# One wait of the wide exponential, and the places of some VectorE work, in a fused attention and token-mixing kernel

## The chip, the cores and the metric

The kernel runs on one core of a Trainium2 chip. A core has engines that run side by side, each through its own list of instructions in order: TensorE (PE; its weight loads are shown apart as PEld), VectorE (DVE), ScalarE (ACT), GpSimd (POOL), and SyncE (SP), which here only issues DMAs. An instruction can wait for semaphores that other engines, DMAs or its own engine raise. Whatever stands behind a waiting instruction on its engine waits as well. The metric is the time of one execution on the device in microseconds (us); lower is better.

## The reference

Two branches on the same x (2048 tokens of 512 channels, fp32) are mixed by a gate for each token:

```python
g = sigmoid((x * gate_w).sum(-1, keepdims=True))
q, k, v = split(x @ wqkv)                       # 32 heads of 16
p = softmax(q @ k.T * 16**-0.5)                 # per head, 2048 x 2048
a = concat_heads(p @ v) @ wo
h = layernorm(x)                                # over channels
u = gelu(h.T @ w1 + b1)                         # over tokens, 2048 -> 1792
b = (u @ w2 + b2).T                             # 1792 -> 2048
out = g * a + (1 - g) * b
```

Everything is fp32. Products are made of two rounded parts, hi and lo, of each factor (hi*hi + hi*lo + lo*hi).

## The kernel before

**Stages.** Until about 280 us the kernel makes v, the keys, half of the queries and the first layer of the token branch. From then to about 1255 us it runs attention, with the rest of the dense work beside it, and then a short end.

**A phase.** Attention is a loop over 128 phases `p`. Four phases (`ph` 0 to 3) make a group of two heads for 1024 queries (32 groups; groups 0 to 15 are the first half of the queries). Each phase computes 16 blocks of scores, 128 keys by 512 queries, numbered `n`. All become exponentials, in three ways:

- SINGLE, n = 0, 2, 4, 6, 8, 9: ScalarE takes each alone from PSUM (`p<-s`, L1043).
- TWO, (10, 11) and (12, 13): ScalarE takes two neighbouring banks at once (`p<-t`, L986, 1024 columns).
- EVAC, n = 1, 3, 5, 7, 14, 15: VectorE copies them to SBUF (`pe<-s`, and `pe<-u` for 14 and 15, L1039), and ScalarE turns all six into exponentials with one instruction, the wide exponential (`pe<-pe`, L1050, 3072 columns; in the last phase two parts of 1024 and 2048).

Then TensorE multiplies the exponentials with v (`av`, L921): first those that were held back in the phase before (the six of EVAC), then the ten of this phase. VectorE adds the result to `ot` (L943). In each phase with `ph` = 0 the group before is finished: its `ot` goes to memory in eight DMAs (`o`, `r`), and a second add (`ot<-t`) belongs to the new group.

**Dense work beside the scores.** A score uses 64 of the 128 rows of the array; the other 64 do a step of a dense product (`dn`, L1031), 12 or 14 steps a phase, one half of the contraction in an even and the other in the odd phase. The dense products are the second layer (16 tiles), 8 late projections of the queries' second half (`late_query`), and 8 tiles of the output projection of the first half (`project`). Each ends in an odd phase with VectorE reading the bank `dn` (`done`, for a late projection `out`, L605); the next phase's first step of `dn` needs that bank again.

**Order.** All five engines run in the order in which the program calls them (`manual_schedule`). In a phase, VectorE does the four copies `pe<-s`, the two `pe<-u`, then `done` of a dense product, a memset of `mark`, which stands for several waits at once, up to two casts of weights (in odd phases), what `on_dve(p, ...)` has put down for that phase (`later`), and then the adds. SyncE's DMAs of `call(p, ...)` are issued at the head of phase p. The tables of numbers below `put_whole` decide at which phase each piece runs. `tc.add_manual_dep(a, b, ...)` makes a wait for the end of b. The wide exponential has such a wait for `pairs_done[1]`, the second pair, the instruction just ahead of it on ScalarE; after it, later instructions need no own wait for that pair.

**Inversions and fetches.** The sums of exponentials go to memory (`r`), come back as `inv`, are inverted on VectorE (`invert`: `turn`, L734 and L735) and go back as `ri` (`put_back`). A fetch (L747) loads `o` and `ri`, multiplies them (`on_dve` at its first number), casts the product to hi (second number) and subtracts for lo (third). `fetch_left` runs four times, between phases 83 and 105; `fetch_right` and `fetch_o` from phase 112 on.

## Time and profile before

| what | value |
|---|---|
| median of 3 runs | 1290.22 us (1289.85 to 1290.26) |
| the profiled execution | 1290.4 us |
| its span in the profile | 1288.5 us |
| TensorE / ScalarE / VectorE / GpSimd busy | 1273.4 / 1084.4 / 854.2 / 199.2 us |
| wide exponentials | 129, the first at 283.5 us |
| granted clock of TensorE over the span | 0.999 |

The profile is of one execution. A timeline row reads: start and duration in us, engine, line of the kernel, operation, tiles written and read with their shapes, how many instructions are merged in the row, and in brackets the idle time of the engine ahead of it and what ended it. A row of waits reads: who waited for whom, us in total, how often, the longest. A row of windows reads, for a stretch: its length, the busy time of PE, PEld, DVE, ACT and POOL with instruction counts, the granted clock, the share of the DMA engines, GB/s. Consecutive instructions of an engine may overlap at their ends, so the time from start to start is what an engine needs for each.

### The profile page before, as it was taken

How to read it: one execution, taken by the hardware profiler on the slowest of the kernel's cores; microseconds unless marked ns; L12 is line 12 of the kernel's file. 1: busy time of each engine (PE TensorE's matmuls, PEld its weight loads, DVE VectorE, ACT ScalarE, POOL GpSimd, SP SyncE). 2: the span in 40 equal slices, each digit the busy share in tenths (PEclk: the TensorE clock that was granted, in tenths of full speed). 3: DMA queues.
4: the chain of work that ended last, by engine and by line, in shares of the span. 5: the costliest groups of instructions: out<-in, count | busy, mean ns of one | idle time of the engine just before them, and what ended most of it. 6: DMA issues, size and time to landing. Idle time of an engine off the chain costs nothing.

```text
span 1288.5 us, 32655 instructions
## 1 busy us (share of the span) xinstructions
PE 1273.4 (99%) x13342; PEld 846.5 (66%) x13342; DVE 854.2 (66%) x1547; ACT 1084.4 (84%) x1405; POOL 199.2 (15%) x316
## 2 busy tenths in 40 slices
PE   9999999999999999999999999999999999999998
PEld 7888888875666666666666666666656656666656
DVE  5675544088767666767667677766776677678873
ACT  4443344279999999999999999999999999999990
POOL 0220444461110101010110101111111111000000
PEclk9999999999999999999999999999999999999999
DMA  3799442253754443634344443444543342266511
GB/s 131 261 330 332 131 124 90 81 135 107 209 126 98 83 96 75 162 77 100 84 100 95 97 95 63 91 96 75 111 99 75 77 97 59 55 163 180 142 57 69
DMA packets 100554, 152.30 MB, mean 118 GB/s; under 512 B 17109, under 2 KB 56171, under 8 KB 96300
## 3 DMA queue, kind: packets, MB, share of 16 engines
q1 hardware_dynamic: 99820, 149.08, 45.0%
q8 instruction: 107, 1.75, 0.6%
q10 hardware_dynamic: 576, 1.05, 0.2%
q14 instruction: 51, 0.42, 0.1%
HBM read 105.39 MB, written 44.68 MB: 116 GB/s over the span
## 4 chain that ended last, share of the span: by engine, by line
PE 92%; DVE 4%; ACT 2%; DMA 1%; issue 1%; SPq 0%; DVEq 0%; ACTq 0%
PE av L921 26%; PE s L1022 19%; PE acc L424 12%; PE t L1022 9%; PE acc L75 8%; PE dn L1031 6%; PE t L921 5%; PE u L1022 3%; PE pa L1105 2%; DVE pe L1039 1%; ACT pe L1050 1%; PE acc L199 1%; ACT p L1043 1%; DVE row L610 0%; DVE row L68 0%
## 5 line engine op out<-in xcount | busy, mean ns | idle before, releaser
L1043 ACT ACTIVATE p<-s 128x512 f32<-128x512 f32 x768 | 388.4, 605 | 5.0 <-PE s L1022 2.8
L1050 ACT ACTIVATE pe<-pe 128x3072 f32<-128x3072 f32 x129 | 354.5, 2749 | 5.1 <-DVE mark L1058 1.0
L1022 PE MATMUL s<-qs,ks 64*128 64x512 f32 x1280 | 335.5, 403 | 3.7 <-DVE ot L943 3.5
L1039 DVE COPY pe<-s 128x512 f32<-128x512 f32 x512 | 318.0, 684 | 5.2 <-PE s L1022 1.6
L1022 PEld LDWEIGHTS s<-qs,ks 64*128 64x128 f32 x1280 | 224.8, 184 | 102.1 <-issue 48.6
L986 ACT ACTIVATE p<-t 128x1024 f32<-128x1024 f32 x256 | 254.3, 1076 | 0.0
L921 PE MATMUL av<-p,v 128*32 128x256 f32 x3880 | 227.2, 379 | 0.0
L1039 DVE COPY pe<-u 128x512 f32<-128x512 f32 x256 | 165.0, 686 | 85.5 <-PE u L1022 73.8
L921 PE MATMUL av<-pe,v 128*32 128x256 f32 x3072 | 192.5, 383 | 0.1
L943 DVE TENSOR_TENSOR ot<-av,ot 128x512 f32<-128x512 f32 (+2 forms) x149 | 91.3, 614 | 145.4 <-PE av L921 144.3
L1031 PE MATMUL dn<-u_hi,w_hi 64*128 64x512 f32 x448 | 182.6, 408 | 4.2 <-DVE mark L1058 4.2
L68 POOL TENSOR_TENSOR w_lo<-w_raw,w_hi 128x512 fp32r<-128x512 f32 (+1 forms) x128 | 153.3, 1204 | 196.6 <-ACT w_hi L67 99.8
L1031 PE MATMUL dn<-u_hi,w_lo 64*128 64x512 f32 x448 | 182.9, 408 | 0.0
L1031 PE MATMUL dn<-u_lo,w_hi 64*128 64x512 f32 x448 | 181.1, 404 | 0.0
L921 PEld LDWEIGHTS av<-p,v 128*32 128x32 f32 x3880 | 126.0, 110 | 83.3 <-issue 0.2
L1022 PE MATMUL t<-qs,ks 64*128 64x512 f32 x512 | 157.1, 423 | 0.0
L921 PEld LDWEIGHTS av<-pe,v 128*32 128x32 f32 x3072 | 86.7, 109 | 83.2 <-ACT p L1043 36.4
L1035 POOL MEMSET token<- 1x1 f32 x128 | 11.4, 89 | 771.9 <-PE dn L1031 693.4
L1022 PEld LDWEIGHTS t<-qs,ks 64*128 64x128 f32 x512 | 79.3, 184 | 55.5 <-ACT p L1043 53.3
L67 ACT CAST w_hi<-w_raw 128x512 fp32r<-128x512 f32 (+1 forms) x67 | 38.0, 569 | 82.4 <-PE acc L424 63.1
L424 PE MATMUL acc<-h_hi,w_hi 128*128 128x512 f32 x224 | 87.9, 392 | 0.0
L424 PE MATMUL acc<-h_hi,w_lo 128*128 128x512 f32 x224 | 87.8, 392 | 0.0
(164 smaller groups left out, 1640.7 us busy)
## 6 DMA issues: line engine op xcount, KB each, us to landing
w_raw<-in_B_w_dram SPq DMA_DIRECT2D x96, 256.0 KB
ks<-kp SPq DMA_DIRECT2D x192, 128.0 KB
qs<-qp SPq DMA_DIRECT2D x256, 64.0 KB
kp<-pc SPq DMA_DIRECT2D x16, 512.0 KB
qp<-pc SPq DMA_DIRECT2D x8, 768.0 KB
qp<-row SPq DMA_DIRECT2D x24, 256.0 KB
v<-v SPq DMA_DIRECT2D x4, 1088.0 KB
x<-in_A_x_dram SPq DMA_DIRECT2D x16, 256.0 KB
```

The lines of the kernel that those rows point to most:

```text
L67: copy(hi, src)
L68: return sub(lo, src, hi.bitcast(F32), ALU.subtract)
L75: nc.tensor.matmul(ps, a, b, start=start and n == 0, stop=stop and n == last)
L424: nc.tensor.matmul(p, a, b, start=first and k == 0, stop=last and k == 2)
L921: mm = nc.tensor.matmul(av[32 * j : 32 * (j + 1), i * QC : (i + 1) * QC], vb[b][:, v_at : v_at + 32], pt[:, h * QC : (h + 1) * QC], start= ...
L943: latest["add"] = nc.vector.tensor_tensor(x, y, x, ALU.add)
L986: pairs_done.append(nc.scalar.activation(pt, twos[low, low + 1], AF.Exp, scale=SCALE))
L1022: nc.tensor.matmul(s, kt[grp][rows_i, c * P : (c + 1) * P], qt[grp][rows_i, qb * NB : (qb + 1) * NB], start=True, stop=True,)
L1031: mm = nc.tensor.matmul(ps, a[half], b[half], start=begin and not second, stop=last and bool(second))
L1039: nc.vector.tensor_copy(pt, s)
L1043: nc.scalar.activation(pt, s, AF.Exp, scale=SCALE)
L1050: done = nc.scalar.activation(x, x, AF.Exp, scale=SCALE)
```

## The change

The order of instructions is the same on TensorE and ScalarE. What differs is two waits on ScalarE and the places of some VectorE operations and a few DMAs.

1. The wide exponential awaits `pairs_done[0]`, the first pair, and the third single (`SINGLE[2]`, n = 4) of the next phase awaits the second pair of the phase before (`earlier`).
2. A late projection's cast (`begin`) is called ahead of the copies of n = 14 and 15; its operation for the absolute value, with the store of that row, comes in the phase after (`finish`).
3. The casts and subtractions of `fetch_left` come one phase after their product; the subtraction of the last weights one phase after their cast; the constants for the end four phases later.
4. The last inversion (`half` 1, k = 3) is called in phase 126 ahead of the copies of n = 14 and 15 (`amid`), no more behind the mark of phase 125; its store comes behind the mark of 126, and the last fetch is issued in phase 127 instead of 126.

```diff
@@ late_query
+        def begin():
+            box.append(out_pool.tile([P, D], F32, name="row", bufs=3))
+            nc.vector.tensor_copy(box[-1].bitcast(F32R), box[2])
+
         def out():
-            ps, cols = box[2], slice((n - 2) * NB, (n - 1) * NB)
-            hi, lo, most_k = (out_pool.tile([P, D], F32, name="row", bufs=3) for _ in range(3))
-            split(hi.bitcast(F32R), lo.bitcast(F32R), ps, nc.vector.tensor_copy, nc.vector.tensor_tensor)
+            ps, hi, cols = box[2], box[-1], slice((n - 2) * NB, (n - 1) * NB)
+            lo, most_k = (out_pool.tile([P, D], F32, name="row", bufs=3) for _ in range(2))
+            nc.vector.tensor_tensor(lo.bitcast(F32R), ps, hi, ALU.subtract)
             nc.vector.tensor_scalar(most_k, ps, most[:, b : b + 1], None, ALU.mult)
+            nc.vector.tensor_reduce(qmax[:, b, n : n + 1], ps, axis=AX.X, op=ALU.max, apply_absolute_value=True)
+            for i, t in enumerate((hi, lo)):
+                nc.sync.dma_start(qp_d[1][b][i, :, cols], t)
+            box.extend((most_k, qp_d[1][b][2, :, cols]))
+
+        def finish():
+            most_k, dst = box[-2:]
             nc.vector.scalar_tensor_tensor(most_k.bitcast(F32R), most_k, -1.0, most_k, ALU.mult, ALU.max)
-            nc.vector.tensor_reduce(qmax[:, b, n : n + 1], ps, axis=AX.X, op=ALU.max, apply_absolute_value=True)
-            for i, t in enumerate((hi, lo, most_k)):
-                nc.sync.dma_start(qp_d[1][b][i, :, cols], t)
+            nc.sync.dma_start(dst, most_k)
+
+        between[out] = begin
@@ load_wq
-        on_dve(at + 2, split, wq[0], wq[1], raw, nc.vector.tensor_copy, nc.vector.tensor_tensor)
+        on_dve(at + 2, nc.vector.tensor_copy, wq[0], raw)
+        on_dve(at + 3, nc.vector.tensor_tensor, wq[1], raw, wq[0].bitcast(F32), ALU.subtract)
@@ invert
-        on_dve(at, turn)
         def put_back():
             nc.sync.dma_start(ri_d[half][k][:n].rearrange("r (a b) -> (r a) b", b=w), t)
-        calls.setdefault(at + 1, []).insert(0, (put_back,))
+        if half and k == ND - 1:
+            amid[at + 1] = [turn]
+            on_dve(at + 1, put_back)
+        else:
+            on_dve(at, turn)
+            calls.setdefault(at + 1, []).insert(0, (put_back,))
@@ put_whole
-        steps, load = what
+        steps, load, *finish = what
         call(2 * at - 2, load)
+        if finish:
+            on_dve(2 * at + 2, *finish)
@@ the table of phases
-        call(p0, fetch_left, k, p0 + 2, p0 + 2, p0 + 2)
+        call(p0, fetch_left, k, p0 + 2, p0 + 3, p0 + 3)
-    on_dve(p0 + 9, end_constants)
+    on_dve(p0 + 13, end_constants)
-    call(LAST - 1, lambda: fetch_o(3, LAST, LAST, LAST, pairs=3))
+    call(LAST, lambda: fetch_o(3, LAST, LAST, LAST, pairs=3))
@@ the loop over n in a phase
+                if n == HELD[-1][0]:
+                    if n_b and second and beside[-1][-1] in between:
+                        between[beside[-1][-1]]()
+                    for what in amid.get(p, ()):
+                        what()
                 if n in EVAC:
...
-                    nc.scalar.activation(pt, s, AF.Exp, scale=SCALE)
+                    one = nc.scalar.activation(pt, s, AF.Exp, scale=SCALE)
+                    if n == SINGLE[2] and p:
+                        tc.add_manual_dep(one.ins, earlier.ins.name, SYNC, reason=EARLY)
@@ behind the loop over n
-            tc.add_manual_dep(done.ins, pairs_done[1].ins.name, SYNC, reason=EARLY)
+            tc.add_manual_dep(done.ins, pairs_done[0].ins.name, SYNC, reason=EARLY)
             evac_done.append(done)
+            earlier = pairs_done[1]
```

ScalarE, from the last pair of one phase to the fourth single of the next, before and then with the change (the waits of each row in brackets):

```order
L986 ACTIVATE p_4542<-t_4527 128x1024 [waits PE_49]
L1050 ACTIVATE pe<-pe 128x3072 [waits DVE_49,Activation_49]
L1043 ACTIVATE p_4621<-s_4615 128x512 [waits PE_49]
L1043 ACTIVATE p_4628<-s_4614 128x512 [waits PE_49]
L1043 ACTIVATE p_4635<-s_4618 128x512 [waits PE_49]
L1043 ACTIVATE p_4642<-s_4612 128x512 [waits PE_49]
```

```order
L1004 ACTIVATE p_4544<-t_4527 128x1024 [waits PE_49]
L1075 ACTIVATE pe<-pe 128x3072 [waits DVE_49,Activation_49]
L1066 ACTIVATE p_4619<-s_4613 128x512 [waits PE_49]
L1066 ACTIVATE p_4626<-s_4612 128x512 [waits PE_49]
L1066 ACTIVATE p_4633<-s_4616 128x512 [waits PE_49,Activation_49]
L1066 ACTIVATE p_4640<-s_4610 128x512 [waits PE_49]
```

No row moved. The wide exponential still waits for its own engine, now for an earlier instruction of it, and the third single has such a wait too.

VectorE, from the last copies of the phase in which a late projection ends into the phase after it (`row<-dn` are the projection's parts, `z<-dn` its greatest value), before and then with the change:

```order
L1039 COPY pe<-s_9462 128x512
L1039 COPY pe<-u_9482 128x512
L1039 COPY pe<-u_9483 128x512
L67 CAST row<-dn 128x512
L68 TENSOR_TENSOR row<-dn,row 128x512
L609 TENSOR_SCALAR row<-dn,most 128x512
L610 SCALAR_TENSOR_TENSOR row<-row 128x512
L611 TENSOR_REDUCE z<-dn 128x1
L1058 MEMSET mark 1x1
L943 TENSOR_TENSOR ot<-av,ot 128x512
```

```order
L1062 COPY pe<-s_9462 128x512
L607 CAST row<-dn 128x512
L1062 COPY pe<-u_9482 128x512
L1062 COPY pe<-u_9483 128x512
L612 TENSOR_TENSOR row<-dn,row 128x512
L613 TENSOR_SCALAR row<-dn,most 128x512
L614 TENSOR_REDUCE z<-dn 128x1
L1084 MEMSET mark 1x1
L961 TENSOR_TENSOR ot<-av,ot 128x512
```

The cast moved ahead of both copies of u, and the operation on `row` alone (now L621) left for the next phase, where it stands behind that phase's mark.

VectorE, phases 125 and 126 around the last inversion (`inv`), before and then with the change:

```order
L791 SCALAR_TENSOR_TENSOR row<-dn,g,row 128x512 [waits DMAHW2_49]
L1058 MEMSET mark 1x1 [waits DVE_49,Activation_49]
L734 TENSOR_SCALAR inv<-inv 96x64 [waits DMAHW6_49]
L735 RECIPROCAL inv<-inv 96x64 [waits DVE_49]
L943 TENSOR_TENSOR ot<-av,ot 128x512 [waits PE_49]
L1039 COPY pe<-s_18273 128x512 [waits PE_49]
```

```order
L961 TENSOR_TENSOR ot<-av,ot 128x512 [waits PE_49]
L1062 COPY pe<-s_18265 128x512 [waits PE_49]
L1062 COPY pe<-s_18266 128x512 [waits PE_49]
L1062 COPY pe<-s_18262 128x512 [waits PE_49]
L1062 COPY pe<-s_18293 128x512 [waits PE_49]
L746 TENSOR_SCALAR inv<-inv 96x64 [waits DMAHW6_49]
L747 RECIPROCAL inv<-inv 96x64 [waits DVE_49]
L1062 COPY pe<-u_18313 128x512 [waits PE_49]
```

The inversion, which waits for a DMA, moved from ahead of an add and the four copies of phase 126 to behind them.

More of the change, by code (lines that the diff above doesn't have):

```diff
@@ L591, in open_wo @@
         wo.extend(o_pool.tile([P, ND, D], F32R, name=f"big{i}") for i in range(2))
-    wq = []
+    wq, between = [], {}
     def late_query(b, n):
@@ L620, in step @@
             return box[2], box[a][:, k, :], xt[n][x][:, k, :], first, last, out if last else None
-        return [(step, k, j) for k in range(ND) for j in range(3)], load
+        return [(step, k, j) for k in range(ND) for j in range(3)], load, finish
     def second_layer(t):
@@ L663, in least_shifts @@
         nc.vector.tensor_copy(flag, ff)
-    calls, later = {}, {}
+    calls, later, amid = {}, {}, {}
     def call(at, *what):
```

## The prediction

> **What bounds the kernel now.** I read the page, then the windows and waits of the long stage, then the timelines of ScalarE, TensorE and VectorE over a few phases.
>
> ```profile
> span 1288.5 us, 32655 instructions
> ...
> PE 92%; DVE 4%; ACT 2%; DMA 1%; issue 1%; SPq 0%; DVEq 0%; ACTq 0%
> ...
> 340.00:1250.00 910.00, 902.90 (x11152) 562.53 (x11152) 643.51 (x1192) 900.38 (x1078) 93.39 (x208) 1.00 0.44 99
> ...
> PEld t L1022 <- ACT p L1043: 50.0, 207, 0.4
> ...
> PEld av L921 <- ACT p L1043: 34.5, 113, 0.4
> ...
> ACT p L1043 <- PE s L1022: 2.8, 8, 0.4
> ```
>
> The chain of waits gives 92% to TensorE. But the ends of matmuls are modelled, and the row of the stage from 340 to 1250 us (engines in the order PE, PEld, DVE, ACT, POOL) shows two full engines: TensorE 902.90 of 910 us and ScalarE 900.38, at a granted clock of 1.00. The waits of that stage tell them apart: TensorE's weight loads wait for a ScalarE exponential 207 times (50.0 us) and 113 times (34.5 us), in nearly all of the 120 phases; ScalarE waits for a score 8 times (2.8 us). ScalarE sets the pace.
>
> ```profile
> 711.05 2.77 ACT L1050 ACTIVATE pe<-pe 128x3072 f32<-128x3072 f32 x1
> 713.73 3.02 ACT L1043 ACTIVATE p<-s 128x512 f32<-128x512 f32 x6
> 716.59 1.99 ACT L986 ACTIVATE p<-t 128x1024 f32<-128x1024 f32 x2
> 718.61 2.77 ACT L1050 ACTIVATE pe<-pe 128x3072 f32<-128x3072 f32 x1
> ...
> 724.15 1.99 ACT L986 ACTIVATE p<-t 128x1024 f32<-128x1024 f32 x2
> 726.16 2.77 ACT L1050 ACTIVATE pe<-pe 128x3072 f32<-128x3072 f32 x1
> ```
>
> From one wide exponential (L1050) to the next is 718.61 - 711.05 = 7.56 us, then 726.16 - 718.61 = 7.55; I use 7.555 as the phase. Start to start it is made of the wide one (713.73 - 711.05 = 2.68), six singles (716.59 - 713.73 = 2.86) and two pairs (726.16 - 724.15 = 2.01). Neighbours overlap: the wide one lasts 2.77 and the next starts after 2.68. One joint does not: the pairs end at 716.59 + 1.99 = 718.58 and the wide one starts at 718.61, a hole of 0.03 us. There it waits for the pair in front of it to end.
>
> ```profile
> 1250.21 2.00 ACT L986 ACTIVATE p<-t 128x1024 f32<-128x1024 f32 x2
> 1252.02 2.92 ACT L1050 ACTIVATE pe<-pe 128x1024 f32<-128x1024 f32 x2
> ...
> L1050 ACT ACTIVATE pe<-pe x129: 1127/2767/2775, 283.5 to 1253.0; 128x3072 f32<-128x3072 f32 x127, 128x1024 f32<-128x1024 f32 x1, 128x2048 f32<-128x2048 f32 x1
> ```
>
> The last phase shows the joint without that wait, since there the evacuated scores go in two parts and only the second waits for a pair. From the first pair to the first part is 1252.02 - 1250.21 = 1.81 us in place of 2.01. And the second part, which awaits an instruction two places ahead of it, as the wide one will after the change, starts at 1253.0, before the first one's end at 1252.02 + 1.13 = 1253.15: such a wait does not empty the engine. From 283.5 to 1252.02 are 127 phases in 968.5 us; 127 x 7.555 is 959.5, so 9.0 us are stalls.
>
> **The change part by part.** *The wide exponential* awaits the first pair, which is over by then. ScalarE's phase becomes 2.68 + 2.86 + 1.81 = 7.35 us: 2.01 - 1.81 = 0.20 less, or 126 x 0.20 = 25.2 us (the last phase had it already), if the others follow. The wait that is moved to the third single of the next phase is for a pair that ended before the wide one ran, 2.68 us and more earlier; the single ahead of it (0.48 start to start) covers its handling. No instruction changes its place on ScalarE. The wide one also awaits VectorE's copies of the scores u:
>
> ```profile
> 721.15 2.48 DVE L1039 COPY pe<-s 128x512 f32<-128x512 f32 x4
> 724.38 1.29 DVE L1039 COPY pe<-u 128x512 f32<-128x512 f32 x2 [0.75 <-PE u L1022]
> ```
>
> They end at 724.38 + 1.29 = 725.67; it would start at 724.15 + 1.81 = 725.96. There are 0.29 us of room.
>
> Can TensorE hold 7.35? Its own chain, where it doesn't wait:
>
> ```profile
> 727.95 0.50 PE L1022 MATMUL s<-qs,ks 64*128 64x512 f32 x1
> ...
> 728.29 0.40 PE L1022 MATMUL s<-qs,ks 64*128 64x512 f32 x1
> ...
> 729.46 0.40 PE L1022 MATMUL s<-qs,ks 64*128 64x512 f32 x1
> ...
> 708.97 0.57 PE L1022 MATMUL u<-qs,ks 64*128 64x512 f32 x2
> 709.47 0.42 PE L921 MATMUL av<-pe,v 128*32 128x256 f32 x4
> ...
> 713.06 0.50 PE L1022 MATMUL s<-qs,ks 64*128 64x512 f32 x1
> ```
>
> First score to second: 728.29 - 727.95 = 0.34. Then, five steps in 1.17, 0.234 a step, and 13 steps to the two scores u: 3.04. From the last u (it ends at 708.97 + 0.57 and lasts 0.39, so starts at 709.15) to the first av 0.32. From there to the next phase's score 713.06 - 709.47 = 3.59. The sum is 7.29 us, 0.06 under ScalarE's 7.35, so TensorE follows with little room. I take 7.35 and 1.0 us in all for phases that miss it. The other end is 7.49: 7.29 and two restarts after a wait that cost 0.34 instead of 0.234; then 0.065 a phase, 8 us, come instead of 25.2.
>
> *The late projections.* In 8 phases VectorE's five operations on a projection push its add, and the copies behind it, back:
>
> ```profile
> 703.05 2.77 ACT L1050 ACTIVATE pe<-pe 128x3072 f32<-128x3072 f32 x1
> ...
> 701.12 1.29 DVE L1039 COPY pe<-u 128x512 f32<-128x512 f32 x2 [0.60 <-PE u L1022]
> 702.32 0.68 DVE L67 CAST row<-dn 128x512 fp32r<-128x512 f32 x1
> ...
> 704.42 0.69 DVE L610 SCALAR_TENSOR_TENSOR row<-row 128x512 fp32r<-128x512 f32 x1
> ...
> 705.64 0.69 DVE L943 TENSOR_TENSOR ot<-av,ot 128x512 f32<-128x512 f32 x1
> ...
> PE dn L1031 <- DVE mark L1058: 4.2, 8, 0.5
> ```
>
> That phase lasts 711.05 - 703.05 = 8.00 us, 0.445 too many, and TensorE waits 8 times (4.2 us) for the bank dn that VectorE still reads. The cast goes into the hole ahead of the copies of u, the L610 operation behind the next phase's mark; three operations stay, and the add can come at 705.64 - 0.68 - 0.69 = 704.27, before its matmuls are done. So 8 x 0.445 = 3.6 us. What could be late next is the first copy of u, by the cast's 0.68 less the hole of 0.60: a tenth a time, inside the 0.29 us of room above. L610's own new place is ahead of an add for which no matmul waits at once. Its store goes to SyncE's queue a phase later, behind two weight loads and ahead of the stores of ot; the rows are read in the second half alone.
>
> *Fetched rows.* Three of the four left fetches stall:
>
> ```profile
> 960.91 2.77 ACT L1050 ACTIVATE pe<-pe 128x3072 f32<-128x3072 f32 x1
> ...
> 962.71 0.84 DVE L1066 CAST v<-row 128x512 fp32r<-128x512 f32 x1
> 963.59 0.69 DVE L1066 TENSOR_TENSOR v<-row,v 128x512 fp32r<-128x512 f32 x1
> ...
> 969.24 2.77 ACT L1050 ACTIVATE pe<-pe 128x3072 f32<-128x3072 f32 x1 [0.26 <-DVE mark L1058]
> ...
> 728.08 0.69 DVE L943 TENSOR_TENSOR ot<-av,ot 128x512 f32<-128x512 f32 x1 [2.42 <-PE av L921]
> ```
>
> 969.24 - 960.91 = 8.33, 0.775 too many. Cast and subtraction (1.5 us) go into the next, even phase, where VectorE is idle for 2.42 us ahead of its add: 3 x 0.775 = 2.3 us. The last weights' subtraction and the constants are moved in the same way; of what then is left of the 9.0 us of stalls I count nothing for them, for the subtraction comes to stand beside another of its size.
>
> *The last inversion.*
>
> ```profile
> 1235.43 2.77 ACT L1050 ACTIVATE pe<-pe 128x3072 f32<-128x3072 f32 x1
> ...
> 1238.79 0.19 DVE L734 TENSOR_SCALAR inv<-inv 96x64 f32<-96x64 f32 x1 [3.03 <-DMA inv<-r]
> ...
> 1239.48 0.62 DVE L943 TENSOR_TENSOR ot<-av,ot 128x512 f32<-128x512 f32 x1
> ...
> 1244.47 2.77 ACT L1050 ACTIVATE pe<-pe 128x3072 f32<-128x3072 f32 x1 [0.26 <-DVE mark L1058]
> ```
>
> VectorE stands 3.03 us at a load, with the add, the four copies, and so scores and exponentials queued behind it. The phase lasts 1244.47 - 1235.43 = 9.04 us, 1.48 too many. Between the next phase's copies the load is in, and 1239.48 - 1238.79 = 0.69 us of work meet a hole of 0.6 to 0.75 (as above). The store of the inverse and the last fetch slip on SyncE's queue too, behind a load of a base row; VectorE takes the fetched rows only after its copies in the last phase, more than a phase later. Gain 1.5 us.
>
> Against this stand phases that just fitted. Each VectorE window shrinks by 0.20:
>
> ```profile
> 1160.77 0.69 DVE L1066 TENSOR_TENSOR e<-o_sum,e 128x512 fp32r<-128x512 f32 x1
> 1161.56 0.69 DVE L943 TENSOR_TENSOR ot<-av,ot 128x512 f32<-128x512 f32 x1
> ```
>
> Here 1161.56 - 1160.77 - 0.69 = 0.10 is left, so 0.10 will be missing. I take nine such phases among those with fetches after 1140 us, an estimate from this row: 0.9 us.
>
> Sum: 25.2 + 3.6 + 2.3 + 1.5 - 0.9 - 1.0 = 30.7 us. The profiled execution took 1290.4 us (its span 1288.5 and 1.9 around it), 0.2 above the median of the runs; from the median, 1290.2 - 30.7 = 1259.5 us.
>
> The Trainium skill, ScalarE: Activation LUTs, section What ACT_TABLE_LOAD costs, states that activations back to back overlap by about 93 ns. This case's trace agrees where a single follows a wide one (2.77 against 2.68) and not at the joint in question, where the last phase has 0.2 from hole and overlap together; the second rival is what that rule would make of it.
>
> **The rivals.** *TensorE takes the pace over*, at 7.40 to 7.49 us. 126 x 0.155 is 19.5, 126 x 0.065 is 8 in place of 25.2 + nothing for missed phases, so the sum is 26 to 14.5 and the time 1264 to 1276. For it: 0.06 us of room, and a restart that costs 0.1. Against: each wait of TensorE is for an exponential that now comes earlier. 14%. *The joint overlaps as the wide one and the single do*, 0.09 us: with the hole 0.12 a phase, 15 us, time 1270. Against: the 1.81 of the last phase. 5%. *The wide one is held by its other wait*, the copies of u, so the change doesn't do what it says: the sum is the 7.4 us of the stalls and the time 1283. Against: 0.29 us of room. 4%. *Slower:* a wait on ScalarE's own count stops it until it is idle, whatever it awaits. Then the third single pays the 0.03 hole and the 0.12 it overlaps now (3.02 for six, 0.48 x 5 + 0.60), the wide one keeps its hole, and 126 x 0.15 = 19 us are lost against 7.4 won: 1302. It decides from 0.06 us a phase on. Against: the second part in the last phase. 3%.
>
> **How the numbers follow.** Forecast 74%, 1256 (all stalls gone, none new) to 1263; rivals 14, 5, 4 and 3%. The range from 1255 to 1270 takes in the second rival and half of the first. A measurement here tells 0.2%, 2.6 us, from no change: faster 0.96, same 0.01, slower 0.03.
>
> **What would show it.** Right: wide to wide 7.35, first pair to wide 1.81; no wait of dn for the mark; no load ahead of the last inversion; TensorE's waits for ScalarE shrunk, few the other way. Wrong: phases of 7.40 and more in which ScalarE waits for s; a wide one released by VectorE; a hole ahead of the third single; VectorE standing at the last fetch in the last phase.

## The result and the profile after

The changed kernel takes 1268.32 us (median of 4 runs, 1267.55 to 1268.68); the kernel before took 1290.24 us beside it (4 runs, 1289.85 to 1290.27). The ratio is 0.983, with a 95% interval from 0.9813 to 0.9847. It is faster, as forecast, and inside the range (1255 to 1270), but 8.8 us above the predicted 1259.5: of 30.7 us, 21.9 came. Line numbers from here on are those of the changed kernel: the wide exponential is L1075, singles L1066, pairs L1004, copies L1062, scores L1040, `dn` L1049, `av` L939, the add L961, `mark` L1084.

From the page after, the span and the chain by engine, then the row of windows for 340 to 1220 us, first of the changed kernel and then of the one before (length; busy time of PE, PEld, DVE, ACT, POOL with counts; granted clock; DMA share; GB/s):

```profile
span 1265.7 us, 32791 instructions
...
PE 98%; DVE 1%; ACT 1%; DMA 0%; issue 0%; SPq 0%
```

```profile
340.00:1220.00 880.00, 879.24 (x11057) 548.65 (x11053) 633.44 (x1181) 879.79 (x1068) 93.46 (x207) 1.00 0.45 102
```

```profile
340.00:1220.00 880.00, 874.01 (x10811) 545.16 (x10815) 622.00 (x1155) 871.87 (x1044) 93.10 (x204) 1.00 0.45 100
```

ScalarE's idle time in this stretch falls from 8.1 us to 0.2. That looks like an engine used to the full, and in most of the stretch it is one. But the gain per phase is smaller than forecast, and the timeline of ScalarE (start, duration) shows why:

```profile
698.89 1.97 ACT L1004 ACTIVATE p<-t 128x1024 f32<-128x1024 f32 x2
700.70 2.81 ACT L1075 ACTIVATE pe<-pe 128x3072 f32<-128x3072 f32 x1
703.36 3.09 ACT L1066 ACTIVATE p<-s 128x512 f32<-128x512 f32 x6
706.22 2.06 ACT L1004 ACTIVATE p<-t 128x1024 f32<-128x1024 f32 x2
708.03 2.90 ACT L1075 ACTIVATE pe<-pe 128x3072 f32<-128x3072 f32 x1
```

Read by starts, this phase is 708.03 - 700.70 = 7.33 us, better than the 7.35 of the forecast. Read by ends, it is (708.03 + 2.90) - (700.70 + 2.81) = 7.42 us. The difference went into the durations: the same instruction "takes" 2.81 us in one phase and 2.90 in the next. The phase stands behind the end of a late query. From the wide exponential two before it on, the starts stand 7.55, 7.56, 7.33, 7.33 and 7.43 us apart (this phase is the third), the ends 7.42, 7.50, 7.41, 7.42 and 7.42. So starts fall back at such a place and run ahead again behind it, by up to 0.35 us over the end of the instruction ahead, while the ends hardly move. Over the kernel the median duration of the wide exponential grows from 2.767 us to 2.982, and in the median plain phase starts too say 7.41. A single phase read by starts is no measure of the pace, and so the sentence ahead of the prediction, that the time from start to start is what an engine needs, does not hold for one phase or one joint. I went through all phases again from end to end of neighbouring instructions. Medians over undisturbed phases (110 before; after, the 99 of the first, second and fourth row of the next table, 16 of them with 12 dense steps), us, worked out from the trace's records of both kernels:

```
end to end          single after wide   4 singles  1st pair's single  pair   pair   wide after pair   phase
before  (110)       0.485               0.488 each  0.488             0.916  0.917  2.800             7.556
after   (99)        0.488               0.490 each  0.489             0.916  0.917  2.646             7.417
```

(The third column of numbers is the last single, the one ahead of the first pair.) The joint that the change opens gave 2.800 - 2.646 = 0.154 us, not the 0.20 that starts showed (2.01 to 1.81), and the phase 0.139. By ends from the first wide exponential to the last, the 127 phases gained 22.0 us (the other 0.8 of the span lies ahead and behind):

| phases | before | after | gained |
| --- | --- | --- | --- |
| 80 plain phases, 14 steps | 7.557 | 7.419 | 11.1 |
| 16 phases of the late queries, 12 steps | 7.552 | 7.418 | 2.1 |
| 8 phases behind a late query | 8.019 | 7.508 | 4.1 |
| 3 phases with fetched rows | 8.306 | 7.414 | 2.7 |
| 15 phases of the output projection, 12 steps | 7.67 | 7.54 | 2.0 |
| first 4, and the last | 7.848, 5.919 | 7.847, 5.840 | 0.1 |

The stalls are gone, as the timeline of VectorE shows at a late query's end and at the last inversion of the changed kernel:

```profile
700.50 0.69 DVE L621 SCALAR_TENSOR_TENSOR row<-row 128x512 fp32r<-128x512 f32 x1
...
701.11 0.68 DVE L961 TENSOR_TENSOR ot<-av,ot 128x512 f32<-128x512 f32 x1
...
1217.44 2.48 DVE L1062 COPY pe<-s 128x512 f32<-128x512 f32 x4
1219.84 0.18 DVE L746 TENSOR_SCALAR inv<-inv 96x64 f32<-96x64 f32 x1
1220.05 0.55 DVE L747 RECIPROCAL inv<-inv 96x64 f32<-96x64 f32 x1
1220.52 1.27 DVE L1062 COPY pe<-u 128x512 f32<-128x512 f32 x2
```

The moved L621 stands in the next phase, and the add behind it is in time; the inversion fills the hole between the copies, with no load ahead of it. The waits of 340 to 1250 us have no row of `dn` for the mark any more; what is left between TensorE, ScalarE and VectorE:

```profile
PEld t L1040 <- ACT p L1066: 37.6, 191, 0.3
PEld av L939 <- ACT p L1066: 37.4, 120, 0.4
...
PEld u L1040 <- DVE pe L1062: 24.4, 114, 0.4
...
ACT o_sum L1179 <- PE pa L1161: 7.0, 1, 7.0
```

ScalarE's first row in that list is of the end of the kernel; in the phases the list shows no wait of it. TensorE's weight loads for the scores `u`, though, now wait 114 times for VectorE's copy. In the kernel before, the same view had:

```profile
PEld u L1022 <- DVE pe L1039: 5.4, 23, 0.4
```

But in the phases of the output projection ScalarE's phase is 1146.33 - 1138.76 = 7.57 us, with a wide exponential that is back at 2.83 and 2.82 us (ends: 7.56), near the 2.77 of the kernel before:

```profile
1138.76 2.83 ACT L1075 ACTIVATE pe<-pe 128x3072 f32<-128x3072 f32 x1
1141.61 3.05 ACT L1066 ACTIVATE p<-s 128x512 f32<-128x512 f32 x6
1144.52 1.97 ACT L1004 ACTIVATE p<-t 128x1024 f32<-128x1024 f32 x2
1146.33 2.82 ACT L1075 ACTIVATE pe<-pe 128x3072 f32<-128x3072 f32 x1
```

TensorE and VectorE in the same phase, changed kernel:

```profile
1141.07 0.50 PE L1040 MATMUL s<-qs,ks 64*128 64x512 f32 x1
...
1143.92 0.41 PE L1040 MATMUL t<-qs,ks 64*128 64x512 f32 x1
1144.38 0.49 PE L1040 MATMUL u<-qs,ks 64*128 64x512 f32 x1
1144.38 0.50 PE L1040 MATMUL t<-qs,ks 64*128 64x512 f32 x1
1144.71 0.39 PE L1040 MATMUL u<-qs,ks 64*128 64x512 f32 x1
1145.04 1.50 PE L939 MATMUL av<-pe,v 128*32 128x256 f32 x24
...
1148.63 0.50 PE L1040 MATMUL s<-qs,ks 64*128 64x512 f32 x1
```

```profile
1141.84 2.48 DVE L1062 COPY pe<-s 128x512 f32<-128x512 f32 x4
```

The phase is 1148.63 - 1141.07 = 7.56 us here too. With 12 dense steps the last scores run in the order 12, 14, 13, 15, two at a time on the two halves of the rows. Score 14 (`u`) goes into the bank of score 7, which the fourth copy frees at 1141.84 + 2.48 = 1144.32; 13 runs beside it and 15 behind it, at 1144.71, and only then, at 1145.04, the product `av`. With 14 steps the order is 12, 13, and then 14 beside 15: only one turn stands behind that wait, not two.

The first four phases gained nothing as a sum, but not each by itself. In two of them ScalarE does one more instruction (L560); these fell from 8.07 to 7.92 and 7.93 us. The first and the fourth rose, from 7.67 and 7.58 to 7.83 and 7.71. There VectorE does work of the first layer (L555 to L557, then L564) ahead of its add and copies, and in both a wide exponential of the changed kernel starts late, by 0.27 and 0.17 us. The first of them:

```profile
290.80 2.77 ACT L1075 ACTIVATE pe<-pe 128x3072 f32<-128x3072 f32 x1 [0.27 <-DVE mark L1084]
293.47 0.62 ACT L560 ACTIVATE big<-big 128x512 f32<-128x512 f32 x1
```

The view names the mark. The copies of `u`, which the wide exponential awaits, end at the same time, 290.70, so they are the likelier cause. That these two phases lost for this reason was not tried in a run of its own.

### The profile page after: what moved, and what is told of

It is laid out like the page before. It is cut to its first block, busy times and chain, and to the rows that moved or that the text cites. A ratio compares the mean times of both kernels' runs of the same rounds, so it can differ in the third digit from the quotient of the medians.

```text
span 1265.7 us, 32791 instructions
## 1 busy us (share of the span) xinstructions
PE 1257.1 (99%) x13342; PEld 838.1 (66%) x13342; DVE 849.1 (67%) x1547; ACT 1071.2 (85%) x1405; POOL 199.3 (16%) x316
## 4 chain that ended last, share of the span: by engine, by line
PE 98%; DVE 1%; ACT 1%; DMA 0%; issue 0%; SPq 0%
PE av L939 31%; PE s L1040 22%; PE acc L424 12%; PE acc L75 8%; PE t L1040 8%; PE t L939 5%; PE dn L1049 5%; PE u L1040 4%; PE pa L1131 2%; PE acc L199 1%; PE acc L268 1%; DVE pe L1062 0%; PE pa L1161 0%; ACT p L1066 0%; DMA wv_raw<-in_A_wqkv_dram 0%; ACT pe L1075 0%
## 5 line engine op out<-in xcount | busy, mean ns | idle before, releaser
L1066 ACT ACTIVATE p<-s 128x512 f32<-128x512 f32 x768 | 406.2, 726 | 0.4
L1075 ACT ACTIVATE pe<-pe 128x3072 f32<-128x3072 f32 x129 | 375.6, 2913 | 0.4 <-DVE mark L1084 0.4
L1040 PE MATMUL s<-qs,ks 64*128 64x512 f32 x1280 | 330.1, 400 | 0.8 <-DVE ot L961 0.8
L1062 DVE COPY pe<-s 128x512 f32<-128x512 f32 x512 | 318.0, 684 | 4.6 <-PE s L1040 1.1
L1040 PEld LDWEIGHTS s<-qs,ks 64*128 64x128 f32 x1280 | 225.8, 184 | 91.8 <-issue 51.9
L1004 ACT ACTIVATE p<-t 128x1024 f32<-128x1024 f32 x256 | 268.6, 1188 | 0.0
L939 PE MATMUL av<-p,v 128*32 128x256 f32 x3880 | 227.1, 379 | 0.0
L1062 DVE COPY pe<-u 128x512 f32<-128x512 f32 x256 | 164.9, 686 | 71.4 <-PE u L1040 61.4
L939 PE MATMUL av<-pe,v 128*32 128x256 f32 x3072 | 192.5, 383 | 0.2 <-ACT pe L1075 0.2
L961 DVE TENSOR_TENSOR ot<-av,ot 128x512 f32<-128x512 f32 (+2 forms) x149 | 91.4, 614 | 148.7 <-PE av L939 147.5
L1049 PE MATMUL dn<-u_hi,w_hi 64*128 64x512 f32 x448 | 181.3, 405 | 0.0
L939 PEld LDWEIGHTS av<-p,v 128*32 128x32 f32 x3880 | 126.0, 110 | 83.3 <-issue 0.2
L1049 PE MATMUL dn<-u_hi,w_lo 64*128 64x512 f32 x448 | 180.7, 403 | 0.0
L1049 PE MATMUL dn<-u_lo,w_hi 64*128 64x512 f32 x448 | 179.8, 401 | 0.0
L1040 PE MATMUL t<-qs,ks 64*128 64x512 f32 x512 | 154.6, 411 | 0.0
L939 PEld LDWEIGHTS av<-pe,v 128*32 128x32 f32 x3072 | 86.8, 109 | 84.1 <-ACT p L1066 39.0
L1040 PEld LDWEIGHTS t<-qs,ks 64*128 64x128 f32 x512 | 80.6, 184 | 45.1 <-ACT p L1066 40.6
```

Source lines behind the costliest of these rows:

```text
L939: mm = nc.tensor.matmul(av[32 * j : 32 * (j + 1), i * QC : (i + 1) * QC], vb[b][:, v_at : v_at + 32], pt[:, h * QC : (h + 1) * QC], start= ...
L961: latest["add"] = nc.vector.tensor_tensor(x, y, x, ALU.add)
L1004: pairs_done.append(nc.scalar.activation(pt, twos[low, low + 1], AF.Exp, scale=SCALE))
L1040: nc.tensor.matmul(s, kt[grp][rows_i, c * P : (c + 1) * P], qt[grp][rows_i, qb * NB : (qb + 1) * NB], start=True, stop=True,)
L1049: mm = nc.tensor.matmul(ps, a[half], b[half], start=begin and not second, stop=last and bool(second))
L1062: nc.vector.tensor_copy(pt, s)
```

## The experiments

Three theories came out of this. **A**: ScalarE sets the 14-step phases, and its price for a wait on the instruction just ahead is 0.14 to 0.154 us, as ends show. **B**: the 12-step phases are set by the order of their last four scores. **C**: the moves of VectorE's work ended the stalls, 7.4 to 7.7 us. The rivals are in each expectation. Where 12 and 14 steps are told apart, phases are from end to end of the wide exponential.

| run | median, us | ratio to before, 95% interval |
| --- | --- | --- |
| changed kernel | 1268.32 | 0.9830 (0.9813 to 0.9847) |
| moves alone (old wait) | 1282.48 | 0.9940 (0.9924 to 0.9955) |
| waits alone | 1279.96 | 0.9919 (0.9904 to 0.9934) |
| own order of the scores | 1266.70 | 0.9816 (0.9802 to 0.9829) |
| shorter wide exponential (one score of six left out) | 1260.77 | 0.9771 (0.9756 to 0.9786) |
| one more wait on the instruction ahead | 1282.86 | 0.9944 (0.9929 to 0.9959) |
| wide exponential in two | 1275.47 | 0.9885 (0.9870 to 0.9901) |
| old end of the late queries | 1274.19 | 0.9877 (0.9862 to 0.9892) |
| three pairs | 1290.98 | 1.0007 (0.9998 to 1.0016) |
| one exponential over four scores | 1310.86 | 1.0159 (1.0145 to 1.0173) |
| own order and shorter wide exponential (one score of six left out) | 1255.62 | one run |

The kernel before took 1290.24, 1290.06, 1290.00 and 1290.41 us beside these runs (the changed kernel; the next four rows; the next four; the last two).

### The moves alone

```diff
-            tc.add_manual_dep(done.ins, pairs_done[0].ins.name, SYNC, reason=EARLY)
+            tc.add_manual_dep(done.ins, pairs_done[1].ins.name, SYNC, reason=EARLY)
...
-                    if n == SINGLE[2] and p:
-                        tc.add_manual_dep(one.ins, earlier.ins.name, SYNC, reason=EARLY)
```

> The changed kernel with the wide exponential waiting for the end of the second pair's exponential again, and no wait ahead of the third single one; all of VectorE's moves stay. Theory A (the new wait is worth 0.158 us in each of the 80 plain phases of 14 scores, and nothing in the phases of 12 scores; the moves end the stalls, 7.6 to 7.7 us): every phase returns to 7.555 us from wide to wide and the time is about 1282.5 us. Rival (the predicted 0.20 us in 126 phases, part of it eaten up by something that the moves brought): more of the gain hangs on the moves than the stalls, and the time is about 1285 us or more, or below 1280 us if the moves also shorten plain phases.

1282.48 us, as theory A and C had it, though A had counted it otherwise: against this run the change's waits are worth some 0.14 us in each of 99 phases, the 12-step phases of the late queries among them, and not 0.158 in 80. The plain phases are back at 7.557. By ends the moves alone gain 3.7 us behind the late queries, 2.2 us at the fetched rows and 1.7 us in the phases of the output projection, with the last inversion.

### The waits alone

```diff
-            tc.add_manual_dep(done.ins, pairs_done[1].ins.name, SYNC, reason=EARLY)
+            tc.add_manual_dep(done.ins, pairs_done[0].ins.name, SYNC, reason=EARLY)
...
+                    if n == SINGLE[2] and p:
+                        tc.add_manual_dep(one.ins, earlier.ins.name, SYNC, reason=EARLY)
```

> The kernel before with the two changed waits alone (the wide exponential waits for the first pair's exponential, the third single one for the second pair's), nothing of VectorE moved. Theory A: plain phases of 14 scores fall from 7.555 to about 7.40 us, phases of 12 scores stay at 7.55, the stalls of the late projections, the fetched rows and the last inversion stay as they were: about 1276 us (14.3 us gained). Rival (the forecast's own term, 0.20 us in all 126 phases, lost in the changed kernel to its moves): 1265 us.

1279.96 us: neither. The 80 plain phases gained 10.8 us as in the changed kernel, so the moves did not eat up the wait's gain. But the stalls grew. The eight phases behind a late query went from 8.019 to 8.31 us. VectorE and ScalarE there, in the run with the waits alone (L1039 copies, L943 add, L1043 singles, L1052 wide):

```profile
393.03 2.48 DVE L1039 COPY pe<-s 128x512 f32<-128x512 f32 x4
...
397.31 0.68 DVE L67 CAST row<-dn 128x512 fp32r<-128x512 f32 x1
...
400.62 0.69 DVE L943 TENSOR_TENSOR ot<-av,ot 128x512 f32<-128x512 f32 x1
...
401.38 2.48 DVE L1039 COPY pe<-s 128x512 f32<-128x512 f32 x4
```

```profile
389.96 3.01 ACT L1052 ACTIVATE pe<-pe 128x3072 f32<-128x3072 f32 x1
...
397.51 2.87 ACT L1052 ACTIVATE pe<-pe 128x3072 f32<-128x3072 f32 x1
400.35 0.60 ACT L1043 ACTIVATE p<-s 128x512 f32<-128x512 f32 x1
401.62 2.59 ACT L1043 ACTIVATE p<-s 128x512 f32<-128x512 f32 x5 [0.67 <-PE s L1022]
```

VectorE's first copy of a phase starts 0.06 us behind the wide exponential's end (393.03 against 389.96 + 3.01 = 392.97). In the kernel before, at the same phase, it started 391.01 + 2.77 - 393.56 = 0.22 us ahead of it:

```profile
391.01 2.77 ACT L1050 ACTIVATE pe<-pe 128x3072 f32<-128x3072 f32 x1
```

```profile
393.56 0.69 DVE L1039 COPY pe<-s 128x512 f32<-128x512 f32 x1
```

The next first copy and ScalarE's next wait in the kernel before:

```profile
401.92 2.48 DVE L1039 COPY pe<-s 128x512 f32<-128x512 f32 x4
```

```profile
402.16 2.56 ACT L1043 ACTIVATE p<-s 128x512 f32<-128x512 f32 x5 [0.34 <-PE s L1022]
```

From first copy to first copy VectorE takes the same with both waits: 401.38 - 393.03 = 8.35 us, and 401.92 - 393.56 = 8.36 in the kernel before; at all eight late queries it is 8.35 or 8.36. So its block of operations sets this stretch either way, and a ScalarE that is quicker ahead of it only waits longer: 0.67 us in place of 0.34. Moves and waits together gain 21.9 us, alone 7.6 and 10.1.

### The old end of the late queries

```diff
-            nc.vector.tensor_tensor(lo.bitcast(F32R), ps, hi, ALU.subtract)
+            split(hi.bitcast(F32R), lo.bitcast(F32R), ps, nc.vector.tensor_copy, nc.vector.tensor_tensor)
             nc.vector.tensor_scalar(most_k, ps, most[:, b : b + 1], None, ALU.mult)
+            nc.vector.scalar_tensor_tensor(most_k.bitcast(F32R), most_k, -1.0, most_k, ALU.mult, ALU.max)
```

`begin` and `finish` are gone with it, and the three stores stand together again.

> The changed kernel with the old end of a late query projection: all five VectorE operations at the end of the phase, as before the change. Theory (VectorE's work is uncovered by more in the quicker phases, as in the run with the new waits alone, where these eight phases took 8.31 us): the phases after a late query go from 7.50 to 8.31 us, 6.4 us more, 1274.7 us. Rival (the move is worth what the stall was in the kernel before, 0.46 us each): 3.7 us more, 1272 us.

1274.19 us, as the theory had it, 5.9 us more than the changed kernel (6.3 by ends): the eight phases took 8.30 us. The edit is worth 6.3 us by ends once the waits are quick, and 3.7 us where they were not.

### Own order of the scores

```diff
-            alone = NSC - (NSC - n_b) // 2
+            alone = NSC - 1
...
-            in_turn = list(range(n_b)) + [n for pair in zip(range(n_b, alone), range(alone, NSC)) for n in pair]
+            in_turn = list(range(NSC))
```

> The changed kernel, with the scores of the phases that have 12 dense steps in the order of those that have 14: scores 12, 13 and 14 on one half of the rows, 15 on the other, in their own order. No score then stands behind the one that waits for VectorE's fourth copy, but the one that runs beside it. Theory B (in 12-step phases the two scores and their restart behind that wait set the period): these phases fall from 7.55 to about 7.41 us, and the time by 31 to 36 times 0.14 us, 4.3 to 5 us, to about 1263.5 us. Rival (another bound holds those phases: the second layer's or the projections' own work on VectorE or their exponentials): they stay at 7.55 and the time at 1268 us, or above it, since two scores more run one after the other.

The phases did what theory B said: 7.42 us in the output projection (from 7.54) and behind the late queries (from 7.51). TensorE in this run, one turn behind the wait and not two:

```profile
1143.27 0.65 PE L1040 MATMUL t<-qs,ks 64*128 64x512 f32 x2
1143.67 0.50 PE L1040 MATMUL u<-qs,ks 64*128 64x512 f32 x2
1144.16 1.50 PE L939 MATMUL av<-pe,v 128*32 128x256 f32 x24
```

The time fell by less than expected, to 1266.70 us (1266.15 to 1266.91), 1.6 us. Two things shrink it. By ends the gain over all phases is 2.5 us, not 4.3 to 5: the expectation counted 31 to 36 phases from start to start, and the late queries' own phases were at 7.42 already, carried by ScalarE's full queue. And of these 2.5 the span shows 0.7: in this profile the first wide exponential starts 0.6 us later (283.5 us against 282.9), and the end behind the last one is 1.3 us longer. What sets these two was not tried. It is the quickest of the kernels that compute all of the reference, by 0.13% of the changed kernel's time, which is less than a measurement here tells from no change; the mechanism rests on the phases, not on that time.

### A shorter wide exponential

```diff
-            for x in ([evac] if p < LAST else [evac[:, :2, :], evac[:, 2:, :]]):
+            for x in ([evac[:, :5, :]] if p < LAST else [evac[:, :2, :], evac[:, 2:, :]]):
```

> The changed kernel with the wide exponential over five of its six scores (2560 instead of 3072 columns), in every phase but the last: the sixth goes into the product without its exponential. ScalarE has some 0.42 us less to do in a phase. Theory C (ScalarE, by its pitch from end to end, sets the 14-step phases' 7.40 us, with no hole left): these phases fall until TensorE's chain holds them, 7.29 us by the forecast's sum, so about 80 times 0.11, 9 us less, 1259 us; the 12-step phases stay at 7.55. Rival D (TensorE's chain, or VectorE's copies, already hold them at 7.40): nothing changes, 1268 us, and ScalarE waits 0.42 us more in each phase.

1260.77 us, 7.6 us less. The 14-step phases fell from 7.419 to 7.335 (median 7.325), the 12-step phases of the projection stayed at 7.54, and those of the late queries did not fall either (7.418 to 7.443). So ScalarE was the bound of the first and not of the second. Now ScalarE waits in each phase, in this run:

```profile
705.65 2.40 ACT L1075 ACTIVATE pe<-pe 128x2560 f32<-128x2560 f32 x1
708.27 3.06 ACT L1066 ACTIVATE p<-s 128x512 f32<-128x512 f32 x6 [0.22 <-PE s L1040]
```

7.325 us is then TensorE's phase with 14 steps, against 7.29 in the forecast's sum. VectorE is close behind: TensorE's weight load for `u` waits for the fourth copy in nearly every phase (118 times from 340 to 1220 us), though the score starts 0.22 to 0.24 us behind the one ahead, as the others do. TensorE's own steps and VectorE's add and copies could not be told apart as what sets the 7.325.

### Both of these

> The run on the order and the run on the shortened wide exponential together: own order of the scores in all phases, and the wide exponential over five of its six scores in all phases but the last (the sixth goes into the product without its exponential). Theory (with ScalarE's work out of the way TensorE's chain holds all phases alike at 7.325 us): phases of 12 and of 14 steps both at 7.32 to 7.33 us, 31 times 0.22 below the shortened exponential alone, 1254 us. Rival: the phases of 12 steps stay at 7.4 or more, so something other than the wait ahead of the two scores holds them.

1255.62 us (one run; expected 1254). The 15 phases of the projection have a median of 7.33 us, the plain ones 7.324: with ScalarE's work out of the way and the scores in their own order, both kinds go alike. That bears out theory B. Three of the fifteen still take 7.60 to 7.69 us. In them VectorE does three adds behind a fetched row's work and starts its copies late (1137.76, 1167.42 and 1197.10 us in this run); the two later ones are at 7.48 and 7.49 in the run on the order alone.

### One more wait on the instruction ahead

```diff
+                    if n == SINGLE[5]:
+                        tc.add_manual_dep(one.ins, single.ins.name, SYNC, reason=EARLY)
+                    single = one
```

> The changed kernel, in which each phase's last single exponential (score 9) also waits for the end of the single one just ahead of it on ScalarE (score 8). Theory (the price of a wait for the instruction just ahead is what it adds between two ends, and ScalarE without such a wait goes by 7.417 us a phase): the ends of these two singles stand 0.64 us apart instead of 0.490 (0.153 more, as the wide exponential's stood 2.799 after the pair's and now stands 2.646), every phase of 14 steps goes to about 7.56 us, the 12-step phases, which wait for TensorE at 7.55, hardly change: 99 times 0.14 to 0.15, 14 to 15 us more, 1282 to 1283 us. Rival (the price is the 0.20 us that starts show, and the forecast failed for another reason): 99 times 0.20, 20 us more, 1288 us.

1282.86 us. The last single's end stands 0.629 us behind that of the one ahead (0.490 without the wait): 0.139 us. By starts it is 0.688 against 0.477, 0.21. The phase goes to 7.556, and the 14.5 us are what the change gained from its wait (14.2), given back. The price is nearly the same at a single and at the wide exponential (0.139 and 0.154), and it is the one between ends.

### The wide exponential in two

```diff
-            for x in ([evac] if p < LAST else [evac[:, :2, :], evac[:, 2:, :]]):
+            for x in ([evac[:, :3, :], evac[:, 3:, :]] if p < LAST else [evac[:, :2, :], evac[:, 2:, :]]):
                 done = nc.scalar.activation(x, x, AF.Exp, scale=SCALE)
-            tc.add_manual_dep(done.ins, pairs_done[0].ins.name, SYNC, reason=EARLY)
+                tc.add_manual_dep(done.ins, pairs_done[0].ins.name, SYNC, reason=EARLY)
```

> The changed kernel with the wide exponential cut into two of three scores each, both after the first pair's wait. Theory (ScalarE's queue never empties, and each instruction there costs its columns plus a fixed part: 0.490 us for 512 columns and 0.917 for 1024, so 0.427 per 512 columns and 0.063 per instruction): 0.063 us more in each phase of 14 steps, 7.48 us, nothing in those of 12: 99 times 0.063, 6.2 us more, 1274.5 us. Rival (another engine holds the phase at 7.417): no change, 1268 us; or the cut lets the first half run earlier and the phase gains.

1275.47 us, 7.2 us more; the two parts' ends stand 1.362 and 1.364 us behind what is ahead of them, 2.726 in place of 2.646. One instruction more costs 0.080 us, a little over the 0.063 worked out from singles and pairs, which read PSUM while the wide one reads SBUF. ScalarE has no room to hide even that. The Trainium skill, Perfetto Trace Analysis, section Optimizing Scalar/DVE Operations, gives a ScalarE instruction a fixed part of about 93 ns on SBUF and 51 ns on PSUM, and advises larger instructions where the engine is full. The order of the two agrees with this trace, the sizes measured here are 80 and 63 ns; the next two runs are about the advice.

### Three pairs, and one exponential over four scores

If one instruction more costs 0.06 to 0.08 us a phase, one less should gain that. Both tries start from the run with the scores in their own order.

```diff
-    EVAC = 1, 3, 5, 7, 14, 15
-    SINGLE = 0, 2, 4, 6, 8, 9
-    TWO = (10, 11), (12, 13)
+    EVAC = 1, 3, 5, 9, 14, 15
+    SINGLE = 0, 2, 4, 6
+    TWO = (7, 8), (10, 11), (12, 13)
```

> The changed kernel with two edits: the scores of all phases in their own order, with 12, 13 and 14 on one half of the rows (as in the run on the order), and scores 7 and 8 exponentiated as a third pair in place of two singles, VectorE copying score 9 in place of score 7. ScalarE then has eight instructions in a phase for the same columns. Theory (columns plus 0.063 us per instruction, ScalarE sets the pace): 7.417 less 0.062 is 7.355 us a phase, still above the 7.325 us at which TensorE held the phases of the shortened exponential; some 115 phases times 0.062, 7.1 us below the run on the order alone: about 1259.6 us. Rival (the later fourth copy, of score 9, holds TensorE back, or the pair waits for its second score): no gain on 1266.7 us, or a loss.

1290.98 us, no faster than the kernel before. The median phase is 7.60 us. The waits of 340 to 1250 us, and ScalarE, in this run (L1004 pairs, L1050 scores, L1085 wide):

```profile
PEld u L1050 <- ACT p L1004: 58.6, 120, 0.5
```

```profile
730.27 2.87 ACT L1004 ACTIVATE p<-t 128x1024 f32<-128x1024 f32 x3
733.28 2.77 ACT L1085 ACTIVATE pe<-pe 128x3072 f32<-128x3072 f32 x1
```

Scores 14 and 15 go into the banks of 7 and 8, and both are now freed by the pair, in every phase; the copies of 14 and 15 end later, and the wide exponential, which awaits them, starts 733.28 - (730.27 + 2.87) = 0.14 us behind the last pair. That is how this trace reads; no run tried the later release by itself.

```diff
-                pairs_done.append(nc.scalar.activation(pt, twos[low, low + 1], AF.Exp, scale=SCALE))
+                pairs_done.append(nc.scalar.activation(pt, four, AF.Exp, scale=SCALE))
...
-                    if n in (TWO[0][1], TWO[1][1]):
+                    if n == TWO[1][1]:
...
-            tc.add_manual_dep(done.ins, pairs_done[0].ins.name, SYNC, reason=EARLY)
+            tc.add_manual_dep(done.ins, one.ins.name, SYNC, reason=EARLY)
```

> The changed kernel with the scores of all phases in their own order (as in the run on the order), and the two pairs' exponentials (scores 10 to 13) made one instruction of 2048 columns over four neighbouring PSUM banks; the wide exponential then waits for the last single one, the next phase's third single one for the instruction over four, and in each group's first phase the second product takes the bank of score 14 in place of that of score 10. ScalarE has eight instructions for the same columns, and no bank that scores 14 and 15 wait for is released later. Theory (columns plus 0.063 us per instruction, the failure with three pairs having come from the later release alone): 7.355 us a phase, some 115 times 0.062, 7 us below the run on the order alone, 1259.6 us; at most TensorE's 7.325 shows. Rival (the wait for all four scores, 10 to 13, or the products that wait for the later end of the larger instruction, cost as much as the saved instruction): 1266 us or more.

1310.86 us, phases of 7.76. ScalarE and TensorE in this run:

```profile
742.91 1.88 ACT L1008 ACTIVATE p<-t 128x2048 f32<-128x2048 f32 x1 [0.30 <-PE dn L1053]
```

```profile
741.68 0.50 PE L1044 MATMUL t<-qs,ks 64*128 64x512 f32 x1 [0.22 <-ACT p L1070]
```

The four scores share one tile, so the first of them waits until all four banks are free (for the fourth single, 0.22 us), and the exponential waits for all four scores (0.30 us). Both tries saved an instruction and lost more by what the larger one must await, or what awaits it. The saved 0.06 us itself could not be seen.

## Why the prediction was right, and where it was not

The time fell inside the stated range, but not in the 1256 to 1263 us that had 74%. The range held because it was drawn to take in rivals, and two of these came true in part; that their sum stayed inside is luck, not the mechanism.

**ScalarE sets the pace: right** for the 14-step phases, and shown by taking work from it (7.417 to 7.325). In the 12-step phases of the projection it holds no longer after the change.

**The wide exponential, 0.20 us in 126 phases, 25.2 us: this is the step that failed.** In the changed kernel it was worth 14.2 us (1282.48 - 1268.32). Two errors are in it, of about 6 and 4 us. *The size.* The 2.01 and the 1.81 are from start to start. By starts the joint did become 1.81, in the median plain phase too; but the sum 2.68 + 2.86 + 1.81 took the other two terms as fixed, and they grew to 2.69 and 2.91, so that the phase is 7.41 by starts as well. Between ends the joint gives 0.154, the phase 0.139; in 99 phases some 0.06 us each are missing. The prediction's own row of the last phase had the price: by ends, the part of 1024 columns stands 1253.15 - 1252.21 = 0.94 us behind the pair, while a full wide exponential, 2.800, less 2048 columns at 0.429 per 512 (0.917 - 0.488, from pairs and singles) would stand 1.08 behind it, 0.14 more. The extra wait at a single shows the same pair of numbers, 0.21 by starts and 0.139 by ends, and the time follows the ends. *The number of phases.* TensorE's chain (forecast 7.29, measured 7.325) was added up for 14 steps alone. The 15 phases of the projection, the 8 behind the late queries and two of the first 4 could not follow, or followed in part: 27 x 0.20 is 5.4 us, of which 1.1 came against the moves alone. The allowance of 1.0 us for this was too small. (Its other end, 7.29 and two restarts of 0.106 more, is 7.50 and not 7.49; nothing else hangs on it.)

**The late projections, 3.6 us:** 3.7 with the old waits, so the size was right; in the quicker kernel the same edit carries 6.3 by ends. **Fetched rows, 2.3 us:** 2.2. **The last inversion, 1.5 us:** 1.7 over all phases of the projection, of which 1.5 in the inversion's own. **Nine phases that just fit, -0.9 us:** not seen in the changed kernel. The phases they were counted in are those that TensorE holds at 7.54, where VectorE has room. In the run with both edits, where nothing holds these phases at 7.54, three phases of that kind show. The last weights and constants, counted at nothing, were not tried apart.

**The rivals.** *TensorE takes the pace over* came true in the 12-step phases, by an order of scores that the forecast had not looked at, and not in the others. *The joint overlaps as the wide one and the single do*, 0.12 us a phase and 1270 us, was nearest in size and time. It was put at 5% because of the 1.81, the very row that misled.

That rival went back to the Trainium skill, ScalarE: Activation LUTs, section What ACT_TABLE_LOAD costs: activations back to back overlap by about 93 ns. Here the starts of this kernel overlap the ends ahead by up to 0.35 us, and an instruction without the wait gains 0.139 to 0.154 between ends, so that rival's 0.12 was nearer than the forecast and still low.

*The wide one is held by the copies of u* happened in two of the first phases alone (0.27 and 0.17 us, by the copies' times). *A wait on ScalarE's own count stops it whatever it awaits* fell: the third single's end stands 0.490 us behind the one ahead, as the others do.

## What to carry to other kernels

Price a wait between neighbours on one engine by the distance of their ends, and over many of them: starts can run ahead of the end of the instruction in front, and one phase read by starts can show a gain that does not exist. Add up the next engine's chain for every kind of phase, with the turns that stand behind its last wait, before a gain is multiplied by the number of phases. Edits that close stalls and edits that quicken the pace can be worth more together than alone, as here (21.9 us against 7.6 and 10.1); test them both ways, and ask of a larger instruction which of its inputs comes last.

## What the runs showed of the hardware

A wait for the instruction just ahead cost ScalarE 0.139 us at a 512-column exponential and 0.154 at a 3072-column one, while starts showed 0.21 and 0.20. A wait for an instruction further ahead cost nothing that ends show: the third single, with such a wait, stands 0.490 us behind the one ahead, as its neighbours without it do. (No run has the full wide exponential without any wait for ScalarE, so there it is not shown apart.) In the 99 undisturbed phases, with no wait of it in the list, ScalarE gave 0.490 us per 512 columns, 0.917 per 1024 and 2.646 per 3072, while the profile's durations for the same instructions grew to 0.78, 1.25 and 3.00.
